# Last stage planned with less lead for input weights, and identity products with a fixed instruction order between attention and experts

## The chip, the cores and the metric

The kernel runs on one core of a Trainium2 chip. The metric is device time in microseconds (us) of one execution. Five engines work side by side, each through its own list of instructions, in order: PE (TensorE, matrix products; its weight loads are listed apart as PEld), DVE (VectorE), ACT (ScalarE), POOL (GpSimd) and SP (SyncE, which here issues every DMA). An instruction may wait on a semaphore for another engine or for a DMA, and then everything behind it in its engine's list waits too.

## The reference, cut to what matters

Causal attention over 4 batches and 12 heads, then a mixture of 8 experts with softmax routing over 32 slots, then a feed-forward layer with the activation h * cos(h). N = 1792 tokens, D = 768.

```python
scores = scale * q @ k.T, masked above the diagonal
attn   = exp(scores - max) / (sum + 1e-9)
x      = (attn @ v) as [1792, 768]

logits = x @ phi                                    # [1792, 32]
d = softmax of logits over the tokens;  slot_input = d.T @ x      # 32 slots
for e in range(8):
    slot_out[e] = maximum(slot_input[e] @ w1[e], 0) @ w2[e]       # 768 -> 1024 -> 768
c = softmax of logits over the slots;   x = c @ slot_out

h = x @ w_in                                        # 768 -> 2048
out = (h * cos(h)) @ w_out                          # 2048 -> 768
```

## The kernel before, in words

**Three stages.** The attention stage goes over 24 pairs of heads (`pair_step`, line 464), 6 pairs to a batch. It is software-pipelined: step t computes the scores of pair t, the value product of pair t-1 and the layout change of pair t-2. Eight steps into a batch the routing of that batch is worked in (`be_rep`, `be_d`, `be_dk`, `be_u`). For the last batch this happens after the last pair, with no attention work left beside it: `be_rep` (line 393) copies the logits over the partitions, `be_d` (397) takes maximum and exponential on DVE and ACT, `be_dk` (412) transposes the exponentials, `be_u` (439) multiplies them with x, and `be_slots` (457) makes `slotT`, the slots' inputs, on which every product of the expert stage rests.

**The expert stage** (lines 734 to 767) streams w1 and w2 as 48 pieces of 1 MB each. For each of two groups of 4 experts there are 12 pieces of w1 (6 for each half of the hidden width; products on line 743) and 12 pieces of w2 (line 758). A piece lies in one of 26 slots of a ring (`NSLOT`); the attention stage holds 7 of the slots, so 19 pieces are loaded under it, and the 7 slots take pieces as they come free. From then on the load of a new piece waits until PE has used the piece that lies in its slot (`next_piece`, 715, `load_piece`, 244). `be_tok` of the last batch (line 418: the softmax over the slots, product on line 424) and `build_ct` (590: its transposed copy `CT`) are also done here. In this stage the order of the instructions on each engine is made by a scheduler from priorities (`PRI`); attention and last stage stand in an order that is fixed by the program (`tc.manual_schedule()`).

**The last stage** computes W = slot_out @ w_in first (so that x is never formed) and then goes through 64 steps (`seq`): step s is one chunk fc of 128 columns of the hidden width for one block of up to 512 tokens. Its tasks are: H (`t_h`, line 812, PE: W times CT), Y, R, S, G (lines 818 to 827, on ACT, DVE, ACT, DVE: range reduction, sine, product), K (830, ACT) and L (833, POOL), which split the result into a high and a low part, and six B tasks (`back`, 835, PE: three products each on lines 840 to 842). The weights come as 64-bit numbers and are decoded: item j = 2c is the input chunk c of w_in, item j = 2c+1 is the chunk c of w_out. An item is loaded (ld, line 662) into one of four raw tiles, scaled by a (ACT, 669) and put together by l, h and s (DVE, 672, 676, 680); after s its raw tile is free for item j+4. For a chunk of w_out, u (ACT, 691) and v (`lo_part`, 704, POOL or DVE) make its high and low part. For w_in, one or two chunks form a group q (`GRP`), and W is made by wm (PE, 781), w4 (ACT, 789), wr (PE, 792), ws (ACT, 796) and wd (DVE, 800); the H tasks of the group's chunks wait for wd.

**The planner** (lines 858 to 967) sets the order of the last stage. It walks through a model of the engines with a cost for each task, and whenever an engine is free it takes the ready task with the smallest key. The key is about the step that needs the task, less an offset. For all that belongs to w_in the key starts from `need[...] - 3.2`, so these tasks compete as if they were due 3.2 steps before the step that uses them. A load is reckoned at 1.87 us and 0.9 us more until it can be used. The plan fixes only the order; on the chip every instruction runs when its semaphores allow. The table `warm` (line 975) puts 6, 5 and 12 products of the identity (`keep_warm`, 709) behind the first wm, wr and H; nothing uses their result.

Of the kernel before, what the change touches and what calls it, by code (L numbers as in the profile page):

```python
# [29 lines left out]
SEQ = ((0, 0, 2), (1, 0, 3), (2, 0, 4), (0, 2, 6), (1, 3, 8), (2, 4, 10), (0, 6, 13), (1, 8, 16), (2, 10, 16), (0, 13, 16), (3, 0, 16))  # L30
GRP = ((0,), (1,), (2, 3), (4, 5), (6, 7), (8, 9), (10, 11), (12, 13), (14, 15))
LD = False
PL = {23: 2, 24: 2, 25: 1, 26: 2}
CFG = {'rm': 2,
# [118 lines left out]
def moe_stack_kernel(ctx: ExitStack, tc: tile.TileContext, qk, v, cst, phi, w1, w2, w_in, w_out, out):  # L153
# [297 lines left out]


    NPRE = NSLOT - 7

    slotT = phs
# [8 lines left out]
    def pair_step(t):  # L464
# [7 lines left out]
        def sc(j, c):  # L472
            if now:
                ex[j, c] = score(t, j, c)
# [15 lines left out]
        if prv:  # L490
# [3 lines left out]
            ev_t(1, "A" if now else "D")  # L494
        if 8 in bo:
            be_rep(bo[8])
        sc(0, 1)
        sc(1, 1)
# [209 lines left out]

    def keep_warm(n):
        for _ in range(n):  # L710
            PE.matmul(bank[3][:, 0:128], lhsT=ident, rhs=ident, start=True, stop=True)

    ex = {}
# [19 lines left out]

    for g in range(2):
        for hf in range(2):
            if (g, hf) == (0, 1):
                be_tok(NB - 1)
                build_ct()
            hb = bank[1 + hf]
            for i in range(6):  # L740
                w = next_piece().rearrange("p (j f) -> p j f", j=4)
                for j in range(4):
                    PE.matmul(hb[32 * j:32 * j + 4, :], lhsT=slotT[:, i, 16 * g + 4 * j:16 * g + 4 * j + 4],
                              rhs=w[:, j, :], start=(i == 0), stop=(i == 5))
            ACT.activation(h1, hb, AF.Relu)
            tb = bank[3 * hf]
            for c in range(4):
                PE.transpose(tb[:, 128 * c:128 * c + 128], h1[:, 128 * c:128 * c + 128], ident)
            DVE.tensor_copy(hT[:, 4 * hf:4 * hf + 4, :].rearrange("p c (j t) -> p c j t", j=4),
                            tb.rearrange("p (c j t) -> p c j t", c=4, j=4)[:, :, :, 0:SPE])  # L750
        for n in range(3):
            sb = bank[4 + n % 2]
            for qd in range(4):
                w = next_piece().rearrange("p (c j f) -> p c j f", c=2, j=4)
                for c in range(2):
                    kc = 2 * qd + c
                    for j in range(4):
                        PE.matmul(sb[32 * j:32 * j + 4, 0:256], lhsT=hT[:, kc, 4 * j:4 * j + 4], rhs=w[:, c, j, :],
                                  start=(kc == 0), stop=(kc == 7))
            ACT.activation(so, sb[:, 0:256], AF.Copy)  # L760
            tb = bank[6]
            if npc[0] == 48:
                keep_warm(2)
            for c in range(2):
                PE.transpose(tb[:, 128 * c:128 * c + 128], so[:, 128 * c:128 * c + 128], ident)
            DVE.tensor_copy(soT[:, 2 * n:2 * n + 2, 16 * g:16 * g + 16].rearrange("p c (j t) -> p c j t", j=4),
                            tb[:, 0:256].rearrange("p (c j t) -> p c j t", c=2, j=4)[:, :, :, 0:SPE])

# [115 lines left out]
    for q, grp in enumerate(GRP):  # L884
        key = need[grp[0]] - 3.2
        n = len(grp)
# [33 lines left out]
    while len(plan) < len(T):  # L920
# [3 lines left out]
        for e in free:  # L924
# [35 lines left out]
            for x in succ.get(t, ()):  # L960
                nd[x] -= 1
                tr_[x] = max(tr_[x], fin + (0.0 if e == "T" and "T" in T[x][0] else LAT[e]))
                if nd[x] == 0:
                    soon.append((tr_[x], x))
        if not moved:
            nxt = [w_ for w_, _ in soon] + [x for x in list(free.values()) + list(port.values()) + [h - 0.0 for h in hbf if h < 1e8] if x > now + 1e-9]
            now = min(nxt)
# [82 lines left out]
```

## Time and profile before

| | us |
|---|---|
| median of 3 runs | 567.7 (565.5 to 568.99) |
| the profiled execution | 568.7 |
| its span, first to last instruction | 566.8 |
| PE busy | 520.8 (92%) |
| DVE, ACT, POOL busy | 362.9, 318.1, 175.7 |
| moved by DMA | 100.28 MB, mean 177 GB/s |

Times in the rows are microseconds from the start of the span. The attention stage ends at about 198, the expert stage at about 279, and the last back product at about 563. The profiled execution is 1.9 us longer than its span and 1.0 us longer than the median.

### The profile page before, as it was taken

How to read it: one execution, taken by the hardware profiler on the slowest of the kernel's cores; microseconds unless marked ns; L12 is line 12 of the kernel's file. 1: busy time of each engine (PE TensorE's matmuls, PEld its weight loads, DVE VectorE, ACT ScalarE, POOL GpSimd, SP SyncE). 2: the span in 40 equal slices, each digit the busy share in tenths (PEclk: the TensorE clock that was granted, in tenths of full speed). 3: DMA queues.
4: the chain of work that ended last, by engine and by line, in shares of the span. 5: the costliest groups of instructions: out<-in, count | busy, mean ns of one | idle time of the engine just before them, and what ended most of it. 6: DMA issues, size and time to landing. Idle time of an engine off the chain costs nothing. (4 is left out here: it accounts for less than half of the span.)

```text
span 566.8 us, 10260 instructions
## 1 busy us (share of the span) xinstructions
PE 520.8 (92%) x3772; PEld 388.6 (69%) x3772; DVE 362.9 (64%) x904; ACT 318.1 (56%) x737; POOL 175.7 (31%) x209
## 2 busy tenths in 40 slices
PE   4999999989999989987677999899999999999997
PEld 2777777767767753323356878687876777888997
DVE  3777777778777734001386868898797995535532
ACT  4888858867876611010267667564656555443552
POOL 1233333313332300000033554264425654222231
PEclk9999999999999968999797999999999999999999
DMA  5477547555646788999843251325136110203301
GB/s 178 165 256 253 183 160 264 172 225 215 201 167 206 263 323 334 422 420 420 346 150 126 68 211 57 130 94 168 56 117 217 57 56 2 111 2 112 112 1 57
DMA packets 23954, 100.28 MB, mean 177 GB/s; under 512 B 2656, under 2 KB 6624, under 8 KB 17760
## 3 DMA queue, kind: packets, MB, share of 16 engines
q1 hardware_dynamic: 23904, 99.63, 47.8%
q8 instruction: 30, 0.49, 0.3%
q14 instruction: 20, 0.16, 0.1%
HBM read 94.11 MB, written 5.51 MB: 176 GB/s over the span
## 5 line engine op out<-in xcount | busy, mean ns | idle before, releaser
L840 PE MATMUL bank<-zg,zhl 128*128 128x512 f32 (+1 forms) x384 | 142.7, 372 | 0.0
L841 PE MATMUL bank<-zg,zhl 128*128 128x512 f32 (+1 forms) x384 | 140.5, 366 | 0.5 <-POOL zhl L704 0.5
L842 PE MATMUL bank<-zg,zhl 128*128 128x512 f32 (+1 forms) x384 | 140.1, 365 | 0.0
L833 POOL TENSOR_TENSOR zg<-zscr,zg 128x512 fp32r<-128x512 f32 (+1 forms) x64 | 81.0, 1266 | 145.0 <-ACT zg L830 98.8
L304 ACT ACTIVATE p<-p,pst 128x320 f32<-128x320 f32 (+3 forms) x168 | 87.6, 526 | 32.8 <-DVE pst L302 30.9
L321 POOL TENSOR_SCALAR p<-p,pst 128x320 f32<-128x320 f32 (+3 forms) x120 | 62.6, 539 | 131.5 <-ACT p L304 116.8
L840 PEld LDWEIGHTS bank<-zg,zhl 128*128 128x128 f32 x384 | 73.1, 190 | 12.7 <-issue 1.2
L841 PEld LDWEIGHTS bank<-zg,zhl 128*128 128x128 f32 x384 | 73.1, 190 | 12.4 <-POOL zhl L704 0.9
L842 PEld LDWEIGHTS bank<-zg,zhl 128*128 128x128 f32 x384 | 72.9, 190 | 12.1 <-POOL zg L833 0.2
L302 DVE CUSTOM_DVE_ANT_0 p<-bank,cs 128x320 f32<-128x320 f32 (+3 forms) x168 | 66.9, 449 | 16.7 <-PE bank L291 12.6
L821 DVE SCALAR_TENSOR_TENSOR zscr<-zscr,bank 128x512 f32<-128x512 int32 (+1 forms) x64 | 39.5, 617 | 39.9 <-ACT zscr L818 39.7
L324 PE MATMUL bank<-cs,p 128*128 128x128 f32 (+1 forms) x456 | 59.8, 278 | 3.1 <-ACT pts L175 2.9
L824 ACT ACTIVATE zscr<-zscr,b_h 128x512 f32<-128x512 f32 (+1 forms) x64 | 42.6, 666 | 29.9 <-DVE zscr L821 29.9
L324 PEld LDWEIGHTS bank<-cs,p 128*128 128x128 f32 (+1 forms) x456 | 49.6, 134 | 11.3 <-issue 9.6
L827 DVE TENSOR_TENSOR zscr<-bank,zscr 128x512 f32<-128x512 f32 (+1 forms) x64 | 39.7, 621 | 25.4 <-ACT zscr L824 25.1
L818 ACT ACTIVATE zscr<-bank,b_q 128x512 int32<-128x512 f32 (+1 forms) x64 | 40.2, 631 | 23.8 <-PE bank L814 23.1
L291 PE MATMUL bank<-qk 64*128 64x192 f32 (+2 forms) x288 | 48.3, 470 | 5.5 <-DVE pst L302 5.5
L830 ACT ACTIVATE zg<-zscr 128x512 fp32r<-128x512 f32 (+1 forms) x64 | 36.8, 575 | 24.1 <-DVE zscr L827 24.0
L704 POOL TENSOR_TENSOR zhl<-uacc,zhl 128x768 fp32r<-128x768 f32 (+1 forms) x12 | 17.9, 1503 | 95.7 <-ACT zhl L691 95.6
L669 ACT ACTIVATE zraw<-zraw 128x768 f32<-128x768 f32 x32 | 29.3, 916 | 32.0 <-DMA zraw<-in_w_in_dram 17.1
L291 PEld LDWEIGHTS bank<-qk 64*128 64x128 f32 x288 | 27.2, 196 | 26.4 <-issue 10.3
L175 ACT ACTIVATE pts<-bank 128x512 f32<-128x512 f32 x71 | 40.5, 591 | 3.9 <-PE bank L324 2.3
(146 smaller groups left out, 701.5 us busy)
## 6 DMA issues: line engine op xcount, KB each, us to landing
w<-in_w_dram SPq DMA_DIRECT2D x48, 1024.0 KB, 7.1
zraw<-in_w_in_dram SPq DMA_DIRECT2D x16, 768.0 KB, 4.7
zraw<-in_w_out_dram SPq DMA_DIRECT2D x16, 768.0 KB, 4.4
qk<-in_qk_dram SPq DMA_DIRECT2D x24, 480.0 KB, 4.4
xk<-in_v_dram SPq DMA_DIRECT2D x12, 256.0 KB, 2.6
out_dram<-zps SPq DMA_DIRECT2D x8, 256.0 KB, 2.0
xts<-in_v_dram SPq DMA_DIRECT2D x12, 128.0 KB, 2.2
lt<-in_v_dram SPq DMA_DIRECT2D x12, 128.0 KB, 2.2
```

The source lines that it names most:

```text
L175: ACT.activation(o, i, AF.Copy)
L291: PE.matmul(sreg(j, c), lhsT=Q(p)[h, q0:q0 + 128], rhs=K(p)[h, 0:ln], start=True, stop=True)
L302: DVE.tensor_tensor_reduce(out=dst, in0=sb, in1=m, scale=-0.125, scalar=3.0e38, op0=ALU.add, op1=ALU.min, accum_out=st_[:, col:col + 1])
L304: return pr(f"exp{j}{c}")(lambda: ACT.activation(dst, dst, AF.Exp, bias=st_[:, col:col + 1], scale=-1.0, accum_out=st_[:, 8 + col:9 + col]))
L321: ENG[CFG["norm"][3 * j + c if c < 3 else 6]].tensor_scalar(dst, dst, st_[:, 24 + col:25 + col], 0.0, op0=ALU.mult, op1=ALU.add)
L324: PE.transpose(out, src, by)
L818: ACT.activation(y_(s).bitcast(I32), hb[:, 0:n_(s)], AF.Identity, bias=b_q, scale=1.0 / (2.0 * math.pi))
L824: ACT.activation(y_(s), y_(s), AF.Sin, bias=b_h, scale=1.0)
L833: eng.tensor_tensor(g_(s)[1], y_(s), g_(s)[0].bitcast(F32), ALU.subtract)
L840: PE.matmul(o, lhsT=wh, rhs=gh, start=first, stop=False)
L841: PE.matmul(o, lhsT=wl, rhs=gh, start=False, stop=False)
L842: PE.matmul(o, lhsT=wh, rhs=gl, start=False, stop=last)
```

## The change

**Between attention and experts.** `keep_warm` moves up in the program, and `pair_step` calls it in the steps behind the last pair: 0 identity products ahead of `be_rep`, 7 behind it, 2 ahead of `be_u` and 2 ahead of `be_slots` (`KW`). They write a PSUM bank that nothing reads any more. The loops of the expert stage stand in `tc.manual_schedule()`, so that the program's order holds on every engine; `be_tok` now stands behind the second piece of w1 and `build_ct` behind the ninth.

**Last stage.** The offset 3.2 becomes 2.2, for the decode of w_in and for the tasks of W. The planner also holds PE, ACT and DVE back from a task when one with a smaller key becomes ready within 0.4 of the task's own cost (`LA`). `SAFE` and `KD` are 0 and change nothing. Costs, latencies and the table `warm` stay.

```diff
+LA = .4
+KW = (0, 7, 2, 2)
...
         if 8 in bo:
+            if not now:
+                keep_warm(KW[0])
             be_rep(bo[8])
+            if not now:
+                keep_warm(KW[1])
...
         if 8 in bo:
+            if not now:
+                keep_warm(KW[2])
             be_u(bo[8], 0)
             if bo[8] == NB - 1:
...
                 be_u(NB - 1, 1)
+                keep_warm(KW[3])
                 be_slots(0)
                 be_slots(1)
...
-    for g in range(2):
-        for hf in range(2):
-            if (g, hf) == (0, 1):
-                be_tok(NB - 1)
-                build_ct()
...
+    with tc.manual_schedule():
+        for g in range(2):
+            for hf in range(2):
+                hb = bank[1 + hf]
+                for i in range(6):
+                    if (g, hf, i) == (0, 0, 2):
+                        be_tok(NB - 1)
+                    if (g, hf, i) == (0, 1, 3):
+                        build_ct()
...
-        key = need[GRP[qof[c]][0]] - 3.2 if k_ == "i" else need[c]
+        key = need[GRP[qof[c]][0]] - 2.2 if k_ == "i" else need[c] - 0
...
-        key = need[grp[0]] - 3.2
+        key = need[grp[0]] - 2.2
...
+                if e in "TAD" and any(w_ < now + LA * eng[e] and T[x][2] < key - KD and e in T[x][0] for w_, x in soon):
+                    continue
```

**Where rows move, PE between attention and experts.** Before: `be_rep` (L395), the transposes (L324), `be_u` (L444), the product of `be_tok` (L424), `be_slots` (L460), then the first pieces of w1 (L743).

```order
L395 MATMUL bank_71<-lt,cs 128x448
L324 MATMUL bank_71<-cs,dT 112x128 x4
L444 MATMUL bank_71<-xk_77,dk 32x128 x12
L444 MATMUL bank_69<-xk_78,dk 32x128 x12
L424 MATMUL bank_71<-cs,lt 112x32 x4
L460 MATMUL bank_64<-pst_87,uacc 128x32 x6
L743 MATMUL bank_65<-w_209,phs 4x512 x4
L743 MATMUL bank_65<-w_285,phs 4x512 x4
```

Now the same engine and place; every line number is higher, by 4 to 16, and L459 is the identity product.

```order
L399 MATMUL bank_71<-lt,cs 128x448
L459 MATMUL bank_67<-cs 128x128 x7
L328 MATMUL bank_71<-cs,dT 112x128 x4
L459 MATMUL bank_67<-cs 128x128 x2
L448 MATMUL bank_71<-xk_77,dk 32x128 x12
L448 MATMUL bank_69<-xk_78,dk 32x128 x12
L459 MATMUL bank_67<-cs 128x128 x2
L468 MATMUL bank_64<-pst_87,uacc 128x32 x6
L756 MATMUL bank_65<-w_209,phs 4x512 x4
L756 MATMUL bank_65<-w_285,phs 4x512 x4
L428 MATMUL bank_71<-cs,lt 112x32 x4
L756 MATMUL bank_65<-w_360,phs 4x512 x4
```

Eleven identity products came in, and the product of `be_tok` went from ahead of `be_slots` to behind the second piece of w1.

**DVE at the start of the last stage.** Before, from the G of step 0 (L827) to the G of step 2. The tile lt holds the first chunk 1 of w_out (item 3), zfb the chunks 2 and 3 of w_in (items 4 and 6).

```order
L827 TENSOR_TENSOR zscr<-bank_70,zscr 128x512
L676 SCALAR_TENSOR_TENSOR zfb<-zraw_2264,zfb 128x768
L800 TENSOR_TENSOR zWS<-bank_71,zWS 32x128
L672 TENSOR_SCALAR zfb<-zraw_2266 128x768
L821 SCALAR_TENSOR_TENSOR zscr<-zscr,bank_70 128x512
L676 SCALAR_TENSOR_TENSOR zfb<-zraw_2266,zfb 128x768
L680 SCALAR_TENSOR_TENSOR zfb<-zraw_2264,zfb 128x768
L827 TENSOR_TENSOR zscr<-bank_70,zscr 128x512
L680 SCALAR_TENSOR_TENSOR zfb<-zraw_2266,zfb 128x768
L821 SCALAR_TENSOR_TENSOR zscr<-zscr,bank_71 128x512
L680 SCALAR_TENSOR_TENSOR lt<-zraw_2267,lt 128x768
L827 TENSOR_TENSOR zscr<-bank_71,zscr 128x512
```

Now the same stretch, with L840 as the G and L695 as the s.

```order
L840 TENSOR_TENSOR zscr<-bank_70,zscr 128x512
L834 SCALAR_TENSOR_TENSOR zscr<-zscr,bank_71 128x512
L695 SCALAR_TENSOR_TENSOR lt<-zraw_2280,lt 128x768
L840 TENSOR_TENSOR zscr<-bank_71,zscr 128x512
L834 SCALAR_TENSOR_TENSOR zscr<-zscr,bank_70 128x512
L687 TENSOR_SCALAR zfb<-zraw_2277 128x768
L840 TENSOR_TENSOR zscr<-bank_70,zscr 128x512
```

The last part of item 3 (s into lt) moved up by two steps' work, and the decode of the chunks 2 and 3 of w_in moved behind it.

**ACT ahead of W's copies for the fourth group (q = 3).** Before, the copy w4 (L789, 256 wide) stands behind the scaling of item 11 (L669 on raw tile 3).

```order
L830 ACTIVATE zg_2580<-zscr 128x512
L669 ACTIVATE zraw_2267<-zraw_2267 128x768
L789 ACTIVATE cs<-bank_71 128x256
L824 ACTIVATE zscr<-zscr,b_h 128x512
L691 ACTIVATE zhl_2587<-uacc 128x768
L830 ACTIVATE zg_2581<-zscr 128x512
L796 ACTIVATE zWS<-bank_71 96x256
L669 ACTIVATE zraw_2265<-zraw_2265 128x768
```

Now w4 is L802, ws L809 and the scaling L684.

```order
L843 ACTIVATE zg_2595<-zscr 128x512
L684 ACTIVATE zraw_2278<-zraw_2278 128x768
L802 ACTIVATE cs<-bank_70 128x256
L865 ACTIVATE zps_2609<-bank_65 128x512
L809 ACTIVATE zWS<-bank_70 96x256
L865 ACTIVATE zps_2609<-bank_67 128x512
```

The scaling of item 13 (raw tile 1) went from behind the group's ws to the place right ahead of its w4, and item 11 is scaled well earlier.

## Rows read from the trace of the kernel before

**Rows 1.** Stretches: length; busy us (count) of PE, PEld, DVE, ACT, POOL; PEclk; DMA share, GB/s.

```profile
204.00:220.00 16.00, 15.17 (x118) 7.74 (x117) 5.24 (x20) 1.80 (x3) 0.00 (x0) 0.58 0.72 262
...
220.00:278.00 58.00, 47.44 (x578) 17.76 (x574) 8.84 (x20) 5.18 (x11) 0.00 (x0) 0.98 1.01 420
...
290.00:308.00 18.00, 12.65 (x63) 9.28 (x64) 11.19 (x16) 11.72 (x19) 6.78 (x5) 0.81 0.39 132
...
308.00:530.00 222.00, 216.10 (x1063) 173.39 (x1062) 167.59 (x231) 127.41 (x205) 93.96 (x67) 1.00 0.28 100
```

**Rows 2.** PE timeline after the attention stage: start, us, engine, line, operation.

```profile
204.54 2.79 PE L444 MATMUL bank<-xk,dk 112*32 112x128 f32 x48 [0.38 <-DVE dk L416]
...
207.26 1.70 PE L424 MATMUL bank<-cs,lt 128*112 128x32 f32 x8
...
208.77 2.75 PE L460 MATMUL bank<-pst,uacc 128*128 128x32 f32 x12
...
211.97 8.08 PE L743 MATMUL bank<-w,phs 128*4 128x512 f32 x48 [0.45 <-DVE phs L462]
...
222.37 5.33 PE L743 MATMUL bank<-w,phs 128*4 128x512 f32 x48
```

**Rows 3.** SP timeline: loads of expert pieces.

```profile
206.11 0.33 SPq L249 DMA_DIRECT2D w<-in_w_dram  x1
...
213.92 0.33 SPq L249 DMA_DIRECT2D w<-in_w_dram  x1
```

**Rows 4.** An earlier block of L444; weight loads of L711, ns min/median/max, then times and shapes.

```profile
168.53 0.86 PE L444 MATMUL bank<-xk,dk 112*32 112x128 f32 x24
...
L711 PEld LDWEIGHTS bank<-cs x50: 186/192/333, 255.8 to 286.8; 128*128 128x128 f32 x50
```

**Rows 5.** DVE timeline: the last update of the slots' sums (L450).

```profile
207.40 0.61 DVE L450 SCALAR_TENSOR_TENSOR uacc<-uacc,st,bank 128x384 f32<-128x384 f32 x1
```

**Rows 6.** PE timeline of the last stage: first B of step 1, an H, B of step 4.

```profile
302.51 0.99 PE L840 MATMUL bank<-zg,zhl 128*128 128x512 f32 x1
...
307.21 0.40 PE L814 MATMUL bank<-CT,zWS 96*128 96x512 f32 x1
...
317.49 0.39 PE L840 MATMUL bank<-zg,zhl 128*128 128x512 f32 x1
```

**Rows 7.** ACT timeline, then POOL's: the parts of chunk 1 of w_out.

```profile
298.79 0.94 ACT L669 ACTIVATE zraw<-zraw 128x768 f32<-128x768 f32 x1 [1.35 <-DMA zraw<-in_w_in_dram]
...
299.62 0.83 ACT L691 ACTIVATE zhl<-lt 128x768 fp32r<-128x768 f32 x1
...
300.53 1.81 POOL L704 TENSOR_TENSOR zhl<-lt,zhl 128x768 fp32r<-128x768 f32 x1 [3.29 <-ACT zhl L691]
```

**Rows 8.** DVE timeline of the last stage's start.

```profile
279.19 0.55 DVE L672 TENSOR_SCALAR uacc<-zraw 128x768 int32<-128x768 int32 x1
...
279.85 0.96 DVE L676 SCALAR_TENSOR_TENSOR uacc<-zraw,uacc 128x768 int32<-128x768 int32 x1
...
296.60 1.45 DVE L680 SCALAR_TENSOR_TENSOR lt<-zraw,lt 128x768 int32<-128x768 int32 x1
...
305.11 0.42 DVE L800 TENSOR_TENSOR zWS<-bank,zWS 32x256 fp32r<-32x256 f32 x1
```

**Rows 9.** The page's groups L821 and L833: busy us, mean ns; idle before, releaser.

```profile
L833 POOL TENSOR_TENSOR zg<-zscr,zg 128x512 fp32r<-128x512 f32 (+1 forms) x64 | 81.0, 1266 | 145.0 <-ACT zg L830 98.8
...
L821 DVE SCALAR_TENSOR_TENSOR zscr<-zscr,bank 128x512 f32<-128x512 int32 (+1 forms) x64 | 39.5, 617 | 39.9 <-ACT zscr L818 39.7
```

**Rows 10.** Waits of PE from 303 to 530: us in total, times, longest.

```profile
PE bank L792 <- ACT cs L789: 2.3, 3, 1.4
```

**Rows 11.** ACT timeline: scaling of item 16, which waits for its load.

```profile
360.01 0.90 ACT L669 ACTIVATE zraw<-zraw 128x768 f32<-128x768 f32 x1 [2.19 <-DMA zraw<-in_w_in_dram]
```

**Rows 12.** Loads issued from 300 to 500: count, KB each, us to landing.

```profile
zraw<-in_w_out_dram SPq DMA_DIRECT2D x12, 768.0 KB, 4.3
```

**Rows 13.** A v on DVE, in three parts: ns min/median/max.

```profile
L704 DVE TENSOR_TENSOR zhl<-lt,zhl x3: 417/418/424, 474.9 to 475.6; 128x256 fp32r<-128x256 f32 x3
```

More of the change, by code (lines that the diff above doesn't have):

```diff
@@ L31 @@
 GRP = ((0,), (1,), (2, 3), (4, 5), (6, 7), (8, 9), (10, 11), (12, 13), (14, 15))
+SAFE = 0.0
+LA = .4
+KD = 0.0
 LD = False
+KW = (0, 7, 2, 2)
 PL = {23: 2, 24: 2, 25: 1, 26: 2}
@@ L450, in be_u, with keep_warm @@
             DVE.scalar_tensor_tensor(u, u, st[:, 9:10], ub[:, 0:384], op0=ALU.mult, op1=ALU.add)
+    def keep_warm(n):
+        for _ in range(n):
+            PE.matmul(bank[3][:, 0:128], lhsT=ident, rhs=ident, start=True, stop=True)
     NPRE = NSLOT - 7
@@ L707, in moe_stack_kernel @@
     npc = [0]
-    def keep_warm(n):
-        for _ in range(n):
-            PE.matmul(bank[3][:, 0:128], lhsT=ident, rhs=ident, start=True, stop=True)
     ex = {}
@@ L732, in next_piece @@
         return t
-    for g in range(2):
-        for hf in range(2):
-            if (g, hf) == (0, 1):
-                be_tok(NB - 1)
-                build_ct()
[L739 to L754, printed above, removed]
-                for c in range(2):
[L756 to L767, printed above, removed]
@@ new lines, in moe_stack_kernel @@
+    with tc.manual_schedule():
[7 more added lines that the diff above has]
+                        build_ct()
+                    w = next_piece().rearrange("p (j f) -> p j f", j=4)
+                    for j in range(4):
+                        PE.matmul(hb[32 * j:32 * j + 4, :], lhsT=slotT[:, i, 16 * g + 4 * j:16 * g + 4 * j + 4],
+                                  rhs=w[:, j, :], start=(i == 0), stop=(i == 5))
+                ACT.activation(h1, hb, AF.Relu)
+                tb = bank[3 * hf]
+                for c in range(4):
+                    PE.transpose(tb[:, 128 * c:128 * c + 128], h1[:, 128 * c:128 * c + 128], ident)
+                DVE.tensor_copy(hT[:, 4 * hf:4 * hf + 4, :].rearrange("p c (j t) -> p c j t", j=4),
+                                tb.rearrange("p (c j t) -> p c j t", c=4, j=4)[:, :, :, 0:SPE])
+            for n in range(3):
+                sb = bank[4 + n % 2]
+                for qd in range(4):
+                    w = next_piece().rearrange("p (c j f) -> p c j f", c=2, j=4)
+                    for c in range(2):
+                        kc = 2 * qd + c
+                        for j in range(4):
+                            PE.matmul(sb[32 * j:32 * j + 4, 0:256], lhsT=hT[:, kc, 4 * j:4 * j + 4], rhs=w[:, c, j, :],
+                                      start=(kc == 0), stop=(kc == 7))
+                ACT.activation(so, sb[:, 0:256], AF.Copy)
+                tb = bank[6]
+                if npc[0] == 48:
+                    keep_warm(2)
+                for c in range(2):
+                    PE.transpose(tb[:, 128 * c:128 * c + 128], so[:, 128 * c:128 * c + 128], ident)
+                DVE.tensor_copy(soT[:, 2 * n:2 * n + 2, 16 * g:16 * g + 16].rearrange("p c (j t) -> p c j t", j=4),
+                                tb[:, 0:256].rearrange("p (c j t) -> p c j t", c=2, j=4)[:, :, :, 0:SPE])
@@ L961, in moe_stack_kernel @@
                 nd[x] -= 1
-                tr_[x] = max(tr_[x], fin + (0.0 if e == "T" and "T" in T[x][0] else LAT[e]))
+                tr_[x] = max(tr_[x], fin + (0.0 if e == "T" and "T" in T[x][0] else LAT[e]) + (SAFE if x[0] in ("H", "wr", "wm") and x[1] >= 2 else 0.0))
                 if nd[x] == 0:
@@ L965, in moe_stack_kernel @@
         if not moved:
-            nxt = [w_ for w_, _ in soon] + [x for x in list(free.values()) + list(port.values()) + [h - 0.0 for h in hbf if h < 1e8] if x > now + 1e-9]
+            nxt = [w_ for w_, _ in soon if w_ > now + 1e-9] + [x for x in list(free.values()) + list(port.values()) + [h - 0.0 for h in hbf if h < 1e8] if x > now + 1e-9]
             now = min(nxt)
```

## The prediction

> **What bounds the kernel now.** I read the stretches first [rows 1]. From 220 to 278 the DMA queues are full (share 1.01, 420 GB/s) while PE is busy for 47.44 of 58 us, so the load of the expert pieces ends that stretch. Just ahead of it, from 204 to 220, the queues are busy for only 0.72: 0.28 of 16 us, that is 4.5 us, of transfer time went unused, and PE ran at a mean granted clock of 0.58, mostly the lower level, 1.2 GHz. From 290 to 308, where the last stage starts, PE is idle for 18 - 12.65 = 5.4 us. From 308 to 530 it is idle for only 222 - 216.1 = 5.9 us at full clock: there PE sets the time. So three places can give or take something: the missing DMA time (A), the start of the last stage (B) and the short waits after it (C). The timelines of the first two follow [rows 2 to 8], then the waits of PE [rows 10].
>
> **A, between attention and experts.** A load of a new piece waits until an old piece has been used [rows 3]: the first load that waits for a product of w1 goes out at 213.92, since that product starts only at 211.97 [rows 2]. On the way there, at 1.2 GHz, stand be_u with 2.79, the product of be_tok with 1.70 and be_slots with 2.75 us. The change does two things here.
>
> It takes the product of be_tok off this way. And its eleven identity products fill PE's wait for DVE and ACT, so that the clock may stay at 2.4 GHz. At that level 24 products of be_u took 0.86 [rows 4], so 48 take 1.72. Be_slots is a chain of weight loads; one of that size takes 186 ns against 333 [rows 4], so 2.75 becomes about 1.54. The last update of the sums ends at 208.01 [rows 5], 0.7 behind be_u's end, and with be_tok gone PE sees this 0.7. The copy behind be_slots leaves 0.45, and I give 0.2 to the four identity products that stand on the way (the seven lie in a wait). So w1 starts at 204.54 + 1.72 + 0.7 + 1.54 + 0.45 + 0.2 = 209.15, 2.8 us earlier. Its first piece takes 5.33 / 6 = 0.89 at full clock, and its load can go out at about 210.3 instead of 213.92. The two loads ahead of it (206.11 is the first) wait for be_u and come some 0.7 earlier; at 420 GB/s each takes 2.5 us, so they last until 210.4 and no gap opens. Of the 4.5 us some 1.0 remains, until be_u lets the first of them go. The saving is 3.5 us.
>
> For it to count, the stage must still end by the loads. The fixed order makes PE wait at each small transpose, where the scheduler had put other pieces between; but PE starts 2.8 us earlier and saves 8.08 - 5.33 = 2.75 more in the first six pieces [rows 2], and it had 58 - 47.44 = 10.6 us of slack. Bounds: 0 if PE's new waits eat it all, -4.5 if all the unused time goes. I take -3.5. Moving build_ct costs nothing: it lies beside loads. If the clock stays at 1.2 GHz only the move of be_tok remains, and be_slots then waits for the update at 208.01: 208.77 - 208.1 = 0.7, and with the earlier load some 0.9.
>
> Against this speaks the Trainium skill, "TensorE: Matmul & The Clock Gate", section "A second HAM failure mode: psum-queue depth-cycling": frequent short idles between groups of products can keep the clock falling and rising. By it the eleven products need not hold the clock, and A would be the 0.9 of the first rival below; the row on 204 to 220 shows a low clock with PE listed as busy for 15.17 of 16 us, so it cannot exclude that.
>
> **B, the start of the last stage.** In the kernel before, step 1 of the back products starts at 302.51, at the low clock [rows 6]. It waits for chunk 1 of w_out: its last decode part runs on DVE at 296.60, behind parts of two later input chunks, then ACT makes the high part at 299.62, behind a scaling that waited 1.35 us for its load, then POOL needs 300.53 to 302.34 [rows 7, 8]. The new order puts that decode part right behind the R of step 1, at about 291.5. ACT's high part then waits only for its place behind four other tasks and one scaling, to about 295.3, and POOL's low part, 1.81, behind an L, is ready near 298: step 1 can start 4.5 us earlier.
>
> But most of this is taken back, because the input chunks 2 and 3 now come later. Step 4 needs H of step 4, and this needs the wd of their group, which ran at 305.11 [rows 8]. Ahead of that wd, DVE had 6 l of 0.55, 10 h and s of 0.96 and 8 R and G of 0.62 [rows 8, 9], with some 1.5 for three small ones 19.4 us in 25.9 from 279.19, so 6.5 of waits. Now it has 7 l, 14 h and s, 8 R and G and some 2.6 of small ones: 24.8. With all the waits wd comes at 310.5, with none at 304.0. I take 309, near the upper end, since loads and POOL still make DVE wait. H follows on PE at about 310. From there Y, R, S, G, K at some 0.62 each, one u (0.83) and a second Y that stand between on ACT, 1.27 for L and some 0.1 to 0.2 for each release make 6.7 [rows 7, 9]: the low part of step 4 is ready at 316.7, and PE, which needs it at the third product, starts the step at 316.3. Before, it started at 317.49 [rows 6]. That is 1.2, and the H of step 7, 0.2, is done by then too. B is -1.4.
>
> Bounds: if step 4 were bound by PE alone, the 4.5 us stay; if each of two decodes comes late by a load (4.3 us [rows 12] where the planner reckons 2.8), it is +3.0. The low clock of the stretch from 290 to 308 (0.81 in the mean [rows 1]) matters little in either order, since the chain over DVE and ACT ends last.
>
> **C, the later groups.** Six groups of w_in follow (q = 3 to 8). PE's waits there are few: the longest for w4 is 1.4 us [rows 10], where ACT held w4 behind a scaling that waited 2.19 us for its load [rows 11]. With one step less of lead the decode comes closer to the use. In the fourth group the scaling of item 13 now stands right ahead of w4 on ACT. Its load lands 1.5 us later than the planner reckons [rows 12], so wr, and all the back products queued behind it on PE, may wait for some 2.9 us. Elsewhere ACT has other work between, or the same order as before. I take 2.9 + 5 x 0.6 = 5.9, the same as now: C is 0. Bounds: -5.9, if no wait remains, and 6 x 2.9 - 5.9 = +11.5.
>
> The order also gives more of the low parts v to DVE: 17 instructions, 12 of them parts of 0.42 [rows 13] and 5 whole ones of about 1, where it had 3 parts: some 9 us more. DVE has 222 - 167.59 = 54 us of idle time from 308 to 530 [rows 1], which covers them; without cover they would cost up to 9. POOL has less to do. The row at 296.60 took 1.45 where 0.96 is usual, while POOL worked [rows 8]. The Trainium skill, "SBUF — State Buffer", section "SBUF: two separate sides", names a port pair that DVE and GpSimd lock from each other for a whole instruction; by it each such v could hold an L back by its own length, up to 17 times, which would be the second rival's direction. The long row agrees.
>
> **The sum.** -3.5 - 1.4 + 0 = -4.9 on the profiled execution of 568.7: 563.8. The median of the runs lies 1.0 below that execution, so I predict 562.8.
>
> **The rivals.**
> First, the identity products don't hold the clock. For it: the low clock lasted through products that were listed as busy. Against it: at full clock the same kinds of products ran through the attention stage. A is then -0.9, the sum -2.3, the time 565.4.
>
> Second, slower: the smaller lead makes ACT wait for loads right ahead of w4 in all six later groups, not one, 2.9 us each, 11.5 in all against the 5.9 - and since PE runs its list in order, all of it is lost. Time: 567.7 - 4.9 + 11.5 = 574.3. For it: loads take 4.3 us and the planner reckons 2.8. Against it: in four groups other ACT work stands between. It decides from the third such group on, when 2 x 1.9 + 1.9 is more than 4.9.
>
> Third, the planner's rule of holding an engine back also clears the later waits: C is -3.5 and B the full -4.5. Time: 567.7 - 3.5 - 4.5 - 3.5 = 556.2. For it: the start at 290 to 308 has 5.4 us of idle PE. Against it: wd comes later by count.
>
> That the change doesn't do what it says is small: the order of rows shows all of it.
>
> **How the numbers follow.** A measurement of this kernel tells about 1% from no change: below 562.0 is faster, above 573.4 slower. Forecast 0.48, its own range 559 to 567: 0.21 faster, 0.27 same. First rival 0.18: 0.02 and 0.16. Third rival 0.20, all faster. Second rival 0.14: 0.09 slower, 0.05 same. So faster 0.43, same 0.48, slower 0.09. The range of 8 in 10 goes from 556.0, through the third rival, to 570.5, which leaves out most of the second.
>
> **What would show it.** A: the DMA share from 204 to 220 rises to about 0.9, the clock there to 0.9 or more, the first piece of w1 starts near 209, and the expert stage ends some 3.5 us earlier. B: step 1 of the back products starts 3 us or more sooner after the end of the experts, wd of the third group later, step 4 about 1.4 sooner. C: PE's idle time over the following 222 us stays near 6. Wrong would be: a low clock and an unchanged start of w1; waits of wr for w4 of over 2 us in three or more groups; or a stage of experts that ends by PE and not by loads.

## The result, and the profile after

The changed kernel takes 560.74 us (median of 4 runs, 558.46 to 561.64) against 567.99 (565.5 to 568.99) for the kernel before on the same chip. The ratio is 0.9878, 95% interval 0.9854 to 0.9902. The profiled execution took 561.64 with a span of 559.9, 6.9 less than before's span.

The stretches after, with the columns of [rows 1]:

```profile
204.00:220.00 16.00, 14.78 (x164) 7.43 (x164) 5.94 (x23) 2.39 (x4) 0.00 (x0) 1.00 0.95 372
220.00:278.00 58.00, 47.61 (x570) 18.93 (x568) 11.52 (x24) 6.97 (x14) 0.00 (x0) 0.91 0.99 409
...
290.00:308.00 18.00, 16.62 (x87) 12.96 (x86) 15.97 (x20) 11.04 (x18) 7.77 (x5) 0.94 0.43 155
308.00:530.00 222.00, 215.54 (x1090) 174.77 (x1090) 169.37 (x244) 128.76 (x208) 75.62 (x54) 1.00 0.27 96
```

From 204 to 220 the granted clock is 1.00 where it was 0.58, and the DMA share 0.95 where it was 0.72. From 220 to 278 the clock is now lower, 0.91 against 0.98, and the mean from 262 to 276 is 0.65. PE waits for the last pieces of w2 there, but in the kernel before it is busy for still less of these 14 us (6.72, now 10.33) at 0.98, so what lowers the clock isn't shown; there the low clock came later, with 0.82 from 278 to 290. From 290 to 308 PE is idle for 1.4 us where it was idle for 5.4. From 308 to 530 it is idle for 6.5, about as before.

PE's timeline after the attention stage, as in [rows 2]; L459 is the identity product, and each product is counted as two:

```profile
200.23 1.02 PE L399 MATMUL bank<-lt,cs 128*128 128x448 f32 x2
201.09 1.72 PE L459 MATMUL bank<-cs 128*128 128x128 f32 x14
203.10 0.65 PE L328 MATMUL bank<-cs,dT 128*112 128x128 f32 x4 [0.29 <-ACT dT L410]
...
204.14 1.52 PE L448 MATMUL bank<-xk,dk 112*32 112x128 f32 x48
205.59 0.71 PE L459 MATMUL bank<-cs 128*128 128x128 f32 x4
206.35 1.53 PE L468 MATMUL bank<-pst,uacc 128*128 128x32 f32 x12
208.32 1.90 PE L756 MATMUL bank<-w,phs 128*4 128x512 f32 x16 [0.45 <-DVE phs L470]
210.15 0.97 PE L428 MATMUL bank<-cs,lt 128*112 128x32 f32 x8
```

The seven products at 201.09 lie in the wait for DVE and ACT, of which 0.29 is left. Be_u takes 1.52 where it took 2.79, be_slots 1.53 where it took 2.75, and the product of be_tok stands behind two pieces of w1.

PE's timeline at the end of the expert stage and the start of the last one. L771 is a piece of w2, L794 wm, L827 H, L853 and L855 the first and third product of a B task:

```profile
271.26 1.89 PE L771 MATMUL bank<-w,dk 128*4 128x256 f32 x16 [0.71 <-DMA w<-in_w_dram]
...
275.01 0.71 PE L794 MATMUL bank<-zfa,dT 128*32 128x128 f32 x12 [0.28 <-DVE dT L779]
...
280.30 0.50 PE L827 MATMUL bank<-CT,zWS 96*128 96x512 f32 x1
280.64 2.84 PE L459 MATMUL bank<-cs 128*128 128x128 f32 x24
...
288.25 0.50 PE L827 MATMUL bank<-CT,zWS 96*128 96x512 f32 x1 [1.57 <-DVE zscr L840]
...
294.31 0.39 PE L853 MATMUL bank<-zg,zhl 128*128 128x512 f32 x1
...
305.77 0.63 PE L827 MATMUL bank<-CT,zWS 96*128 96x512 f32 x2
...
310.80 0.39 PE L853 MATMUL bank<-zg,zhl 128*128 128x512 f32 x1
...
311.87 0.50 PE L855 MATMUL bank<-zg,zhl 128*128 128x512 f32 x1 [0.44 <-POOL zg L846]
```

The first wm is the marker between the stages: 275.01 here, 279.33 in the kernel before, so 4.3 us are gained by then (0.34 of them in the attention stage, since be_rep starts at 200.23 and started at 200.57). From the marker, step 1 of the back products (294.31) starts after 19.3 us, before after 23.2; step 4 (310.80) after 35.8, before after 38.2 [rows 6]. From there to the end of the span it is 249.1 and was 249.3. So 6.9 = 4.3 + 2.4 + 0.2. This is one execution of each kernel; other executions divide the gain otherwise, as shown below.

DVE's timeline of the last stage, the rows that answer to [rows 8] (first decode part, item 3's s, wd of the third group), and with them the s of input chunk 1 (zfa), which the experiments come back to:

```profile
274.87 0.55 DVE L687 TENSOR_SCALAR uacc<-zraw 128x768 int32<-128x768 int32 x1
...
278.73 0.96 DVE L695 SCALAR_TENSOR_TENSOR zfa<-zraw,zfa 128x768 int32<-128x768 int32 x1
...
286.63 0.95 DVE L695 SCALAR_TENSOR_TENSOR lt<-zraw,lt 128x768 int32<-128x768 int32 x1
...
304.30 0.42 DVE L813 TENSOR_TENSOR zWS<-bank,zWS 32x256 fp32r<-32x256 f32 x1 [0.63 <-ACT zWS L809]
```

Item 3's s comes 11.8 us after the first decode part and came 17.4 after it; the wd comes after 29.4 and came after 25.9. The waits of PE from 303 to 530, as in [rows 10] (us in total, times, longest); L805 is wr:

```profile
PE bank L827 <- DVE zWS L813: 2.9, 2, 2.0
PE bank L805 <- ACT cs L802: 2.1, 2, 1.4
PE bank L827 <- DVE zscr L840: 1.2, 2, 0.8
PE bank L794 <- DVE zscr L840: 1.1, 1, 1.1
PE bank L855 <- POOL zg L846: 0.4, 1, 0.4
```

### The profile page after: what moved, and what is told of

Its sections match the earlier page's. It is cut to its first block, busy times and chain, and to the rows that moved or that the text cites. A ratio compares the mean times of both kernels' runs of the same rounds, so it can differ in the third digit from the quotient of the medians.

```text
span 559.9 us, 10301 instructions
## 1 busy us (share of the span) xinstructions
PE 516.5 (92%) x3794; PEld 387.3 (69%) x3794; DVE 369.7 (66%) x918; ACT 318.6 (57%) x737; POOL 159.2 (28%) x195
## 4 chain that ended last, share of the span: by engine, by line
PE 51%; DMA 19%; DVE 13%; ACT 12%; issue 3%; SPq 0%; ACTq 0%; DVEq 0%
DMA w<-in_w_dram 10%; PE bank L853 8%; PE bank L854 8%; PE bank L855 8%; PE bank L295 7%; PE bank L328 5%; ACT p L308 5%; DMA zraw<-in_w_in_dram 5%; DMA zraw<-in_w_out_dram 4%; ACT pts L179 3%; DVE zscr L840 2%; PE bank L827 2%; PE bank L363 1%; DVE zfa L695 1%; PE bank L390 1%
## 5 line engine op out<-in xcount | busy, mean ns | idle before, releaser
L853 PE MATMUL bank<-zg,zhl 128*128 128x512 f32 (+1 forms) x384 | 142.4, 371 | 0.0
L855 PE MATMUL bank<-zg,zhl 128*128 128x512 f32 (+1 forms) x384 | 140.2, 365 | 0.4 <-POOL zg L846 0.4
L846 POOL TENSOR_TENSOR zg<-zscr,zg 128x512 fp32r<-128x512 f32 (+1 forms) x64 | 81.6, 1278 | 155.4 <-ACT zg L843 124.3
L853 PEld LDWEIGHTS bank<-zg,zhl 128*128 128x128 f32 x384 | 73.0, 190 | 12.7 <-issue 1.4
L855 PEld LDWEIGHTS bank<-zg,zhl 128*128 128x128 f32 x384 | 72.9, 190 | 12.7 <-POOL zg L846 0.9
L854 PEld LDWEIGHTS bank<-zg,zhl 128*128 128x128 f32 x384 | 73.0, 190 | 11.4
L840 DVE TENSOR_TENSOR zscr<-bank,zscr 128x512 f32<-128x512 f32 (+1 forms) x64 | 39.6, 621 | 22.0 <-ACT zscr L837 21.8
L684 ACT ACTIVATE zraw<-zraw 128x768 f32<-128x768 f32 x32 | 28.9, 910 | 23.4 <-DMA zraw<-in_w_in_dram 15.6
L719 POOL TENSOR_TENSOR zhl<-uacc,zhl 128x768 fp32r<-128x768 f32 x4 | 8.8, 2204 | 98.6 <-ACT zhl L706 98.6
```

What stands on the lines that cost most here:

```text
L840: DVE.tensor_tensor(y_(s), hb[:, 0:n_(s)], y_(s), ALU.mult)
L846: eng.tensor_tensor(g_(s)[1], y_(s), g_(s)[0].bitcast(F32), ALU.subtract)
L853: PE.matmul(o, lhsT=wh, rhs=gh, start=first, stop=False)
L854: PE.matmul(o, lhsT=wl, rhs=gh, start=False, stop=False)
L855: PE.matmul(o, lhsT=wh, rhs=gl, start=False, stop=last)
```

## Experiments

Two questions were open. Between attention and experts: do the identity products make the gain, through the clock, or the fixed order with be_tok moved? In the last stage: does the smaller lead make it, or the rule that holds an engine back? Each ratio is against the kernel before on the same chip; its median there was 567.36 for e1 to e4, 568.02 for e5 to e8, 567.85 for e9 to e11 and 568.34 for e12. A gain in us is (1 - ratio) times that median. In the diffs, "- 3.2 (both places)" stands for the two lines of the planner that hold the lead, of which only the offset is shown, and "..." for lines left out.

**e1, the fixed order alone** (diff against the changed kernel; the plan is the old one).

```diff
-KW = (0, 7, 2, 2)
+KW = (0, 0, 0, 0)
-LA = .4
+LA = 0.0
-- 2.2 (both places)
+- 3.2 (both places)
```

> The kernel before with one part of the change: the fixed order of the expert stage, with be_tok behind the second piece and build_ct behind the ninth, but no identity products and the old plan of the last stage. Theory 1 (the clock does most of the work between attention and experts): the granted clock falls to 1.2 GHz behind the wait for the exponentials as before, w1 starts near 211, the loads gain only some 1 us, time 566 to 567.5, ratio about 0.998. Rival (the order does it, the identity products nothing): the expert stage ends some 4 us earlier as in the changed kernel, ratio about 0.993.

566.65 us, ratio 0.9982 (0.9959 to 1.0004): about 1.0 us, not told apart from nothing. Its profiled execution, the fastest of twelve (565.59), went otherwise than expected: the clock was at its lower level for only some 3 us (0.92 in the mean from 204 to 220), w1 starts at 208.85, and the first wm stands at 274.76, as early as in the change. So this one trace alone would speak for the rival, and the times of e1 and e3 have to decide.

**e2, everything between attention and experts, old plan** (e1 with KW as in the change).

```diff
-KW = (0, 0, 0, 0)
+KW = (0, 7, 2, 2)
```

> The kernel before with all that the change does between attention and experts (identity products and fixed order), and the old plan of the last stage. Theory 1: the first B starts as long after the experts as before, the expert stage ends 4.3 us earlier, ratio 0.992 to 0.993, time about 563.7. Rival (the two parts need each other, since an earlier end of the experts meets loads of the last stage that come no earlier): a gain of 2 us or less, ratio 0.996 or more.

564.42 us, ratio 0.9947 (0.9924 to 0.9970), 3.0 us, less than expected. W1 starts at 207.98.

**e3, the eleven identity products alone**, in the kernel before (the product of be_tok stays ahead of w1).

```diff
             be_rep(bo[8])
+            if not now:
+                keep_warm(7)
...
+            if not now:
+                keep_warm(2)
             be_u(bo[8], 0)
...
+                keep_warm(2)
                 be_slots(0)
```

> The kernel before with the eleven identity products alone; the expert stage keeps the scheduler's order, with be_tok ahead of be_slots. Theory 1: the clock from 204 to 220 stays at 2.4 GHz, w1 starts 1 us later than in the changed kernel (be_tok's product at full clock), the load queues lose some 2 us where the kernel before lost 4.5; gain some 3 us, ratio about 0.995. Rival (the order does it): the start of w1 gains less than 1 us, ratio 0.998 or more.

563.83 us, ratio 0.9951 (0.9926 to 0.9975), 2.8 us. The stretch from 204 to 220 of e3:

```profile
204.00:220.00 16.00, 15.50 (x175) 8.40 (x177) 7.96 (x26) 2.40 (x4) 0.00 (x0) 1.00 0.92 369
```

The clock is at 1.00 and the DMA share at 0.92 with the products alone. E1 and e3 ran on the same chip, beside the same runs of the kernel before: nine of e3's twelve times lie below the fastest of e1's. So the products make the gain. The fixed order adds nothing to the time that can be measured on top of them (0.9947 against 0.9951).

The way from be_rep to the first product of w1 shows the parts. It takes 8.1 us in the seven profiles with the products in the wait and the fixed order (after, e2, e7 to e11; 8.08 to 8.10), 8.9 in e3, 9.0 in e1, and 9.5 to 11.4 in the four with neither (before, e4, e5, e6).

**e4, the plan alone** (lead and hold rule in the kernel before).

```diff
-- 3.2 (both places)
+- 2.2 (both places)
...
+                if e in "TAD" and any(w_ < now + .4 * eng[e] and T[x][2] < key and e in T[x][0] for w_, x in soon):
+                    continue
...
```

The line left out last lets the planner's time step only to moments still ahead; it belongs to the hold rule and stands in the changed kernel too.

> The kernel before with the new plan of the last stage alone (lead 2.2 and the rule that holds an engine back). Theory 1: the expert stage ends at 279 as before, step 4 of the back products starts some 2.5 us earlier after it, the later groups wait for as long in sum; ratio about 0.9955, time 565.4. Rival (the plan gives all that the earlier loads don't, because the stage's start was the whole loss): ratio 0.990 or less.

562.96 us, ratio 0.9916 (0.9893 to 0.9939), 4.8 us, about twice what was expected. With e2 the product is 0.9863, inside the interval of the whole change: the two parts add up. The gain at the start of the stage isn't one of the clock: with 0.97 from 278 to 290 and 0.83 from 290 to 308, step 4 of e4 starts 36.0 us after the first wm, and in e1 and e3, with 1.00 and 0.81 and the old plan, 38.3.

**e5, the smaller lead alone, and e6, the hold rule alone**, in the kernel before. e5 has the two offsets of e4's diff, e6 the rest.

> The kernel before with the lead of 2.2 alone in the planner (no rule that holds an engine back; nothing changed between attention and experts). Theory 2 (the lead makes the gain at the start of the last stage, since the decode of chunk 1 of w_out no longer stands behind that of later input chunks): step 1 of the back products starts about 4 us sooner after the experts, ratio about 0.993. Rival (the rule of holding back makes it): ratio 0.998 or more.

> The kernel before with the rule that holds an engine back for a task with a smaller key, and the old lead of 3.2. Theory 2: the input chunks still come first, step 1 of the back products still starts 23 us after the first wm, ratio 0.997 to 1.002. Rival: step 1 starts 4 us sooner as in the changed kernel, ratio 0.993 or less.

e5: 568.19 us, ratio 0.9990 (0.9970 to 1.0010). e6: 562.54 us, ratio 0.9904 (0.9880 to 0.9928). The rule makes the whole gain of the plan, and the smaller lead none. PE's waits from 303 to 530 in e5 (L814 is H, L781 wm, L792 wr there), then the wait of H for wd in the kernel before:

```profile
PE bank L814 <- DVE zWS L800: 3.4, 5, 1.6
PE bank L781 <- DVE zscr L827: 2.4, 2, 1.7
PE bank L792 <- ACT cs L789: 1.5, 2, 0.8
```

```profile
PE bank L814 <- DVE zWS L800: 0.4, 1, 0.4
```

Less lead does start step 4 earlier (36.1 us after the first wm instead of 38.2), but then H waits for wd five times, and the way from step 4 to the end grows from 249.3 to 251.7. The stretch from 308 to 530, of e5 and then of e6:

```profile
308.00:530.00 222.00, 213.94 (x1061) 171.68 (x1061) 168.84 (x235) 126.40 (x203) 84.21 (x59) 1.00 0.28 98
```

```profile
308.00:530.00 222.00, 216.61 (x1089) 175.29 (x1089) 168.77 (x244) 127.42 (x205) 73.91 (x53) 1.00 0.29 100
```

PE is idle for 8.1 us in e5 and for 5.4 in e6. Both movements of the last stage that I had forecast are the lead's: in e5 item 3's s comes 9.1 us after the first decode part and step 1 starts 17.7 after the first wm (17.4 and 23.2 in the kernel before), and the third group's wd comes late, after 29.2 (25.9). In e6 the s comes after 18.6, step 1 after 22.0 and the wd early, after 23.0. The gain came with e6, that is, without either.

**e7, the identity products of the last stage spread out**, in the changed kernel. The twelve behind the first H take PE for 2.84 us (the row at 280.64) while ACT waits for wr of the second group.

```diff
-    warm = {("wm", 0): 6, ("wr", 0): 5, ("H", 0): 12}
+    warm = {("wm", 0): 6, ("wr", 0): 5, ("H", 0): 2, ("wr", 1): 6, ("H", 1): 6, ("H", 2): 6}
```

> The changed kernel with other identity products at the start of the last stage: 2 instead of 12 behind the first H, and 6 each behind the second wr and the second and third H. In the changed kernel the second wr stands behind the twelve, and ACT waits 2.21 us for it with six tasks behind. Theory 3 (that wait is on the path): the first B starts some 2 us sooner after the first wm, wd of the third group 1 to 1.5 us sooner, ratio about 0.9855 to the kernel before, against 0.988 of the changed kernel. Rival (loads and DVE set the start of step 4): no gain, ratio 0.988.

558.02 us, ratio 0.9825 (0.9793 to 0.9857). Step 4 starts 33.9 us after the first wm instead of 35.8, and the clock from 278 to 290 and from 290 to 308 is 1.00 in both (0.95 and 0.94 in the changed kernel). The interval overlaps that of the change at its edge, so the 3.0 us between the two ratios (0.0053 x 568) are likely, not certain; and the edit moves the twelve products and raises the clock at once, which no run separates.

**e8, a load reckoned with its real duration**, in the changed kernel.

```diff
-    LAT = dict(T=.24, A=.17, D=.1, P=.1, DMA=.9)
+    LAT = dict(T=.24, A=.17, D=.1, P=.1, DMA=2.4)
```

> The changed kernel with one number of the planner changed: a load counts as usable 2.4 us after its transfer instead of 0.9, so 4.3 us in all, which is what the loads of the last stage take. The plan then puts the scalings of items 8 and 13 behind the w4 that they stood ahead of. Theory 4 (scalings that wait for loads hold W's copies back): the waits of PE for w4, 2.1 us in two places, fall to under 1, and the waits for wd of 2.9 fall too; ratio 0.984 to 0.986. Rival (the waits only move to the scaled items' own users): ratio 0.988, the same as the changed kernel.

557.36 us, ratio 0.9814 (0.9789 to 0.9839). PE's waits from 303 to 530 and the stretch from 308 to 530 in e8:

```profile
PE bank L827 <- DVE zscr L840: 1.9, 2, 1.6
PE bank L827 <- DVE zWS L813: 1.0, 3, 0.5
PE bank L855 <- POOL zg L846: 0.3, 1, 0.3
```

```profile
308.00:530.00 222.00, 219.19 (x1118) 178.22 (x1117) 172.82 (x243) 132.56 (x214) 82.23 (x61) 1.00 0.28 97
```

The waits of wr for w4 (2.1 us in the change) are gone, and PE is idle for 2.8 us instead of 6.5. By the ratios that is 3.6 us (0.0064 x 568), and from step 4 to the end it is 3.8 (245.3 against 249.1). The edit lets the planner order the whole stage anew, and one value was tried; that the true duration is the best one isn't shown.

**e9, both**, and from there **e10 with the old lead** and **e11 without the hold rule**.

```diff
 e10 against e9
-- 2.2 (both places)
+- 3.2 (both places)
 e11 against e9
-LA = .4
+LA = 0.0
```

> The changed kernel with both edits that helped alone: the identity products spread at the start of the last stage, and loads reckoned at 4.3 us in the planner. Theory 5 (the first acts before step 4, the second after it, so they add): first wm to step 4 some 33.5 us, PE idle for about 3 us from 308 to 530, ratio about 0.977 to the kernel before. Rival (the first only brings PE sooner to the same waits): ratio 0.981 as with the loads alone.

> As the run with both edits, but with the old lead of 3.2 for all that belongs to w_in. Theory 5 (the rule of holding an engine back makes the gain, the lead itself nothing): the same ratio within 0.003, about 0.977 to 0.980. Rival (with loads reckoned right, less lead pays): ratio 0.983 or more.

> As the run with both edits, but without the rule that holds an engine back. Theory 5: the later groups wait again, PE idle for 6 us or more from 308 to 530, ratio about 0.985. Rival (what hurt the lead alone were the loads reckoned too short, so that the rule is not needed once they are right): ratio 0.977 to 0.980.

e9: 554.24 us, ratio 0.9763 (0.9741 to 0.9785); the steps of e7 and e8 taken together would give 0.9761. e10: 552.60 us, ratio 0.9736 (0.9708 to 0.9763), the best found; it is not told apart from e9, so the smaller lead brings nothing here either. e11: 558.31 us, ratio 0.9824 (0.9800 to 0.9849): without the rule 0.6% is lost. The stretch from 308 to 530 of e10, then of e11:

```profile
308.00:530.00 222.00, 220.52 (x1155) 182.53 (x1155) 164.35 (x240) 132.53 (x215) 86.88 (x65) 1.00 0.28 97
```

```profile
308.00:530.00 222.00, 221.16 (x1143) 181.75 (x1143) 172.16 (x246) 133.13 (x217) 88.64 (x63) 1.00 0.28 97
```

e11 is idle for 0.8 us there, the least of all, where 6 or more was expected. In its profiled execution the loss lies at the start of the stage, as this table of markers shows (us; worked out from the timelines and spans):

| kernel | hold rule | lead | first wm to fourth H | first wm to step 4 | step 4 to the end |
|---|---|---|---|---|---|
| before | no | 3.2 | 15.9 | 38.2 | 249.3 |
| e5 | no | 2.2 | 17.0 | 36.1 | 251.7 |
| e6 | yes | 3.2 | 13.3 | 35.2 | 248.4 |
| after | yes | 2.2 | 13.2 | 35.8 | 249.1 |
| e11 | no | 2.2 | 20.0 | 37.9 | 241.8 |
| e9 | yes | 2.2 | 12.1 | 33.5 | 245.7 |
| e10 | yes | 3.2 | 11.8 | 35.3 | 242.6 |

In every kernel with the rule the fourth H comes 11.8 to 13.3 us after the first wm, in every one without it 15.8 to 20.0. What is left of this at step 4 differs: with the rule step 4 comes 2.9 us earlier in e6 than in the kernel before and 4.4 earlier in e9 than in e11, but only 0.3 earlier in the change than in e5, where 2.6 come behind step 4. And e11 takes back 3.9 of its 4.4 behind step 4: its profiled execution, the fastest of its four (555.91, the others 558.07 to 558.72), has a span only 0.6 longer than e9's. So the table shows what the rule does to the start, and the times that it pays; where the 0.6% went in the other three executions of e11 no trace shows.

Where the late fourth H begins is seen on DVE in e11:

```profile
274.31 0.55 DVE L687 TENSOR_SCALAR uacc<-zraw 128x768 int32<-128x768 int32 x1
...
277.21 0.95 DVE L691 SCALAR_TENSOR_TENSOR zfa<-zraw,zfa 128x768 int32<-128x768 int32 x1
278.08 0.55 DVE L687 TENSOR_SCALAR lt<-zraw 128x768 int32<-128x768 int32 x1
...
280.26 0.69 DVE L834 SCALAR_TENSOR_TENSOR zscr<-zscr,bank 128x512 f32<-128x512 int32 x1 [1.31 <-ACT zscr L831]
280.87 0.95 DVE L695 SCALAR_TENSOR_TENSOR zfa<-zraw,zfa 128x768 int32<-128x768 int32 x1
```

Behind the h of input chunk 1 (277.21), DVE turns to item 3 (lt), then waits 1.31 us for the R of step 0, and does the s of chunk 1 last; it ends 281.82 - 274.31 = 7.5 us after the first decode part. With the rule DVE leaves lt alone for the short while in which this s becomes ready, and it ends 4.8 us after the first part (278.73 + 0.96 - 274.87 in the changed kernel, 4.8 to 4.9 in all kernels with the rule; 6.8 in the kernel before and 7.5 in e5 and e11). In the kernel before it is not the order alone: lt comes first there too, for 0.55, but of the 2.0 us more, 1.2 are the s itself, which took 2.15 us where it takes 0.96 now, while the low part (v) of the first chunk of w_out ran on POOL:

```profile
283.83 2.15 DVE L680 SCALAR_TENSOR_TENSOR zfa<-zraw,zfa 128x768 int32<-128x768 int32 x1
...
283.10 2.07 POOL L704 TENSOR_TENSOR zhl<-uacc,zhl 128x768 fp32r<-128x768 f32 x1 [88.49 <-ACT zhl L691]
```

With the rule the s starts just ahead of that v (278.73, and 278.78 on POOL, in the changed kernel). Wm and wr of the second group and the H tasks of the steps 1 to 3 stand behind that s. In e11 the plan also puts two B tasks of step 0 ahead of the second H on PE.

**e12, the eleven identity products ahead of be_rep** instead of in the waits, all else as in the change.

```diff
-KW = (0, 7, 2, 2)
+KW = (11, 0, 0, 0)
```

> The changed kernel with its eleven identity products all ahead of be_rep, so that PE's wait for the exponentials behind be_rep is idle again, with the same work in sum. Theory 1 (they act by filling that wait, which keeps the clock up): the granted clock falls to 1.2 GHz at about 204 for 3 to 14 us, as in the three profiles without them, be_u takes 2.7 instead of 1.5 us, the time lies 1 to 4 us above the changed kernel, ratio 0.990 to 0.995. Rival (more products anywhere near keep the clock up): no fall of the clock, ratio 0.988 or 0.989, the 0.6 us of the products themselves.

563.39 us, ratio 0.9916 (0.9886 to 0.9945), the same as e4, which has no identity products there; the interval overlaps that of the change (0.9854 to 0.9902). PE's timeline of e12, then its stretch from 204 to 220:

```profile
199.88 2.62 PE L459 MATMUL bank<-cs 128*128 128x128 f32 x22
202.33 0.92 PE L399 MATMUL bank<-lt,cs 128*128 128x448 f32 x2
205.10 0.65 PE L328 MATMUL bank<-cs,dT 128*112 128x128 f32 x4 [1.85 <-ACT dT L410]
206.13 2.16 PE L448 MATMUL bank<-xk,dk 112*32 112x128 f32 x48 [0.39 <-DVE dk L420]
208.34 2.77 PE L468 MATMUL bank<-pst,uacc 128*128 128x32 f32 x12
211.56 3.60 PE L756 MATMUL bank<-w,phs 128*4 128x512 f32 x16 [0.45 <-DVE phs L470]
```

```profile
204.00:220.00 16.00, 14.01 (x104) 7.28 (x108) 4.45 (x16) 1.22 (x4) 0.00 (x0) 0.59 0.72 266
```

The same eleven products, moved in front of the wait, leave the wait of 1.85 us open, and the clock falls to its lower level during be_u: be_slots takes 2.77 again, w1 starts at 211.56, and the DMA share is 0.72, as in the kernel before. So in this execution the products ahead of the wait did not hold the clock. The time of e12 doesn't show it as well: the products delay be_rep by 2.2 us (it starts 2.94 us after the group of products ahead of it starts, 0.70 in the change), where 0.6 was expected of them, and that alone is as much as lies between the two ratios (0.0038 x 568 = 2.2 us). From be_rep to w1 it is 9.2 us, and 8.1 in the change. Three of the six executions had a higher mean clock than the one traced (last section). That the products act by lying in the wait, and not by being more, rests on this one trace, beside the eight with a filled wait.

## Why the prediction was right, and where it was off

**The time.** 560.74 was measured, 562.8 predicted, inside the range and inside the forecast's own range. The sign and the main mechanism held. The gain was 7.1 on the profiled execution (568.7 to 561.64) where the sum said 4.9, and 1.2% by the ratio, just past the bound of 1%; a chance of 0.43 stood on that side.

**A, predicted -3.5.** Its steps came out nearly one by one: be_u 1.52 (I said 1.72), 0.69 from there to be_slots (0.7), be_slots 1.53 (1.54), 0.44 to w1 (0.45), nothing beyond that for the four identity products on the way (0.2). W1 starts at 208.32 (209.15), the first load that waits for it goes out at 209.42 (210.3), and the DMA time unused from 204 to 220 fell to 0.05 x 16 = 0.8 us (1.0). The stage still ends by its loads: its last piece waits 0.71 for its DMA. The trace has -4.3, 0.34 of it in the attention stage; by the ratio of e2 it is -3.0. There is luck in that trace: from be_rep to the first wm the kernel before took 78.8 us, the longest of the four profiles with the old order and no products (e4, e5, e6: 76.3 to 76.6). Their mean is 77.0, that of the eight with products in the wait 73.5 (72.7 to 75.4): -3.5. The first rival, a clock that isn't held, is what the profile of e12 shows. Its price, 0.9 for the move of be_tok alone, was not put to the test: e1 gave 1.0, not told apart from nothing, with a clock that fell for a short while only. The rule that I weighed there, of the Trainium skill, "TensorE: Matmul & The Clock Gate", section "A second HAM failure mode: psum-queue depth-cycling", did not decide this stretch: the short idles that remain between the groups (0.29 and 0.45) went with a granted clock of 1.00 in the changed kernel. It isn't excluded either: in e11, with the same order there, the clock was low from about 209.3 to 212.8, behind be_slots.

**B, predicted -1.4.** The two opposite movements were there and sized well. Step 1 came 3.9 us earlier after the first wm (4.5 predicted), bound by the 18 products of step 0 itself, whose last ends as it begins. The wd of the third group came 29.4 us after the first decode part (309 - 279.19 = 29.8 predicted). H of step 4 followed 30.8 after the first wm (30.7). What was mis-sized is the last link, 6.3 from H to the start of step 4: it took 310.80 - 305.77 = 5.0, and PE then waited 0.4 for the low part ahead of the third product. That low part was there 311.87 - 305.77 = 6.1 after H, where I had 6.7, and PE had begun the step earlier than it needed to. So B was -2.4 in this trace. Three executions of the new plan (after, e4, e12) have 35.9 in the mean from the first wm to step 4, four of the old plan (before, e1, e2, e3) 38.05: -2.2.

**C, predicted 0.** In the one trace it is -0.2 and the idle time is 6.5, as forecast. Over the same seven executions, though, the way from step 4 to the end is 248.0 in the mean against 250.5, so -2.5, and with B -4.7, which agrees with e4 (-4.8). This is the term that was off. Counted from the start of step 4 to the end of the span, PE's idle time explains 1.2 of the 2.5 (9.2 against 10.4 in the mean), and the rest is busy time, 238.8 against 240.1 with one product fewer (1293 against 1294), at a granted clock of 0.99 to 1.00; what makes it shorter isn't shown. The parts v that went to DVE cost nothing that shows on POOL: its L took 1278 ns in the mean and 1266 before.

**What I had wrong is the reason for the plan's gain.** I argued both B and C from "one step less of lead". By e5 the lead is worth nothing: what it gains at the start it gives back in waits for wd. The hold rule, which I had only in the third rival, makes the gain (e6): 2.9 at the start and 0.9 behind it in e6's trace against the kernel before, but 0.3 and 2.6 in the change's against e5 (the table). So the forecast came near the time by a reason that the runs don't bear out: the two movements that I added up for B are the lead's, and the lead pays nothing. That rival priced C at -3.5, nearer than my 0; its full -4.5 for B did not come, since the wd was late as counted.

**The second rival's mechanism is real, its price was too high.** Wr waits for w4 only twice (2.1 us, at most 1.4), not in all six groups. But a load that takes 4.3 us and is reckoned at 2.8 goes with such waits: with the planner told so they are gone, and the time is 3.6 us less (e8).

## What to carry to other kernels

A wait of PE that stands ahead of a chain of small products is worth filling with products of no use, if the chain lets loads go: here they held the clock when they lay in the wait (e3) and not when they stood ahead of it (the profile of e12), and the gain is read from the DMA share of that stretch, not from PE's busy time. Where a planner takes the best ready task, it is worth trying to let it look a fraction of a task ahead before it starts a long one, and to give it measured durations of the loads; here the first was worth 1.0% and the second 0.6%, while shifting a due time was worth nothing. A change of two parts is to be taken apart on the chip before its gain is ascribed to one of them.

## What the runs showed that was not expected

The stretch at the lower clock is not the same from execution to execution, as far as times and mean clocks tell. Of six executions of e12, three with a mean granted clock of 0.972 to 0.979 took 564.4 to 566.0 us and three with 0.987 to 0.991 took 561.4 to 562.4. Profiles without products in the wait showed 0.58 (before), 0.79 (e4) and 0.68 (e5, e6) from 204 to 220, though PE's order there is the same in these four, 0.92 in e1 and 0.59 in e12. With the products in the wait, seven of eight profiles showed 1.00, and e11 showed 0.89: they make the fall rarer, they don't exclude it. What parts the two groups without exception is be_u: it took 1.52 us in all eight, and 2.2 to 2.8 in all six without them.
